# A convolution and feed-forward kernel: its first weight matrix loaded by channel group into 128 partitions, and sixteen closing matmuls left out

## The chip, the cores and the metric

The kernel runs on one core of a Trainium2 chip. The metric is the device time of one execution in microseconds (us). Before the change it is 2172.01 us, the median of three runs that lie between 2171.13 and 2172.34 us. TensorE (PE) does the matmuls, VectorE (DVE) and ScalarE (ACT) the elementwise work, GpSimd (POOL) and SyncE (SP) issue transfers here, and 16 DMA engines move the data.

## What is computed

```python
def _attn_ref(x, weight):                 # x: 8 x 4096 x 192, weight: 8 x 7
    w = softmax(weight, axis=-1)          # one causal filter of 7 taps for each of 8 heads
    # out[b, s, head, :] = sum over k of w[head, k] * x[b, s - 6 + k, head, :]

def _moe_ref(x, w_in, w_out):             # x: 32768 x 192, w_in: 192 x 2048, w_out: 2048 x 192
    h = x @ w_in
    g = h * (1.0 / (1.0 + np.exp(-1.702 * h)))
    return (g @ w_out).astype(np.float32)
```

`w_in` and `w_out` come as 64-bit floats, so the kernel has to turn them into 32-bit floats itself, from two 32-bit words for each number.

## The kernel before, in words

**Steady state.** The 32768 tokens are done in 32 rounds ("big") of 1024 tokens: two halves of 512 tokens in the two halves of the partitions. A round has a first product (x times `w_in`, lines L212 to L247), a gelu on ACT (L236), and a second product with `w_out` (L596, matmuls at L522), which is written as a long plan of forms that saves multiplications. For accuracy the first product takes three passes, over a high part, a low part and a difference of x (`xh`, `xl`, `xd`) with matching parts of the weights (`wh`, `wl`, and what is streamed through `ring`).

**The first round is special** (`first_step`, L713). The weights are not ready when it starts, so it works on four parts of `w_in`, each with 512 columns of the 2048: part i holds column blocks 2i and 2i+1 of 256 columns, one in partitions 0 to 63, the other in partitions 64 to 127. The 192 channels lie as three groups k of 64, side by side in each partition. `load_w_in(i)` (L324) loads part i into `raw[i]`, a region of the tile `g`; for part 0 it is called twice, for the left and the right half of the columns.

Each part then goes through the same steps. On DVE and ACT: `take` (L381, L382 on DVE; it is the first to read the loaded words), `clamp` (L387, L388 on ACT), `join` (L396, L401 on DVE), `rounded_in` (L409 on DVE). Part 0 is used as it is by `plain` (matmuls at L706). Parts 1 to 3 go on through `top` (ACT, L434), `rest` (DVE, L437), `spread` (ACT, L444) and `differ` (DVE, L448), and are used by `quick` (matmuls at L697). PE takes the products in 16 groups; groups 4i to 4i+3 belong to part i, and of these the last two need x with its two partition halves exchanged.

**The exchanges** (L687) are transfers from SBUF to SBUF that swap the two halves of the partitions: `own` and `xt` (x itself), later `xl` into a region of `wh`, and `xd` into a region of `wl`. Channel group 2 of `own` itself comes through such an exchange, so `xh`, `xl` and `xd` wait for one too.

**What sets the order.** The order of each engine is the order of the code. All the loads of `w_in`, all the exchanges, the later loads of `w_out` (L332) and the puts of weights to memory (L458) are issued by SP, in this order: x, `load_w_in(0)` (left, then right half), `load_w_in(1)`, the exchanges of `own` and `xt`, `load_w_in(2)`, `load_w_in(3)`, the exchange of `xl`, the exchange of `xd`, a load of `w_out`, the puts, more loads of `w_out`. On DVE, `take` of part 2 stands ahead of `rest` of part 1, and `take` of part 3 stands ahead of `join` of part 2.

**The end.** After the last round 16 matmuls follow (L902 to L909) whose results nobody reads: twelve of 128 rows by 512 columns and four that use half of the rows.

Of the kernel before, what the change touches and what calls it, by code (L numbers as in the profile page):

```python
# [10 lines left out]
U32 = mybir.dt.uint32  # L11
# [5 lines left out]
def kernel(  # L17
# [9 lines left out]
    nc = tc.nc  # L27
# [8 lines left out]
    NC = D // R  # L36
# [23 lines left out]
    halves = [slice(0, R), slice(R, P)]  # L60
# [23 lines left out]
    def flat_g(r):  # L84
        return g[:, r].rearrange("p n o i t -> p (n o i t)")
# [32 lines left out]
    xh, xl, xd = (consts.tile([P, 2 * NC, T], F32R, name=f"x{i}") for i in "hld")  # L118
# [63 lines left out]
    wh = consts.tile([P, NF // 2, NC, 2, P], F32R)  # L182
# [27 lines left out]
    KS = (1, 2, 0)  # L210
# [84 lines left out]
    raw = [flat_g(r)[:, 2 * PART * i : 2 * PART * (i + 1)] for r, i in ((0, 0), (1, 0), (2, 0), (2, 1))]  # L295
# [21 lines left out]
    w_in_v = moe_w_in.bitcast(U32).rearrange("(k q) (j f) -> j q k f", q=R, j=N_W)  # L317
# [4 lines left out]
    SETS = ((0, 4), (1, 5), (2, 4), (3, 5), (1, 2), (6, 7), (4, 5), (6, 7))  # L322

    def load_w_in(i, cols=slice(0, 4 * P)):  # L324
        for o in range(2):
            nc.sync.dma_start(  # L326
                out=raw[i][halves[o], :].bitcast(U32).rearrange("p (k f) -> p k f", k=NC)[:, :, cols],
                in_=w_in_v[2 * i + o][:, :, cols],
            )

    def load_w_out(i):
# [7 lines left out]
    for r in range(2):  # L339
        load_w_in(0, slice(2 * P * r, 2 * P * (r + 1)))  # L340
    load_w_in(1)

    nc.gpsimd.memset(sel, 1.0)
    for c in range(NC):
        part = sel[:, c, :].rearrange("i (h q) -> i h q", h=2)
        for sign in (1, -1):
            nc.gpsimd.affine_select(
                out=part,
                in_=part,
# [363 lines left out]
    def first_step(tiles):  # L713
# [34 lines left out]
        for i in range(2, N_IN):  # L748
            load_w_in(i)
# [123 lines left out]
    for big in range(1, N_BIG):  # L873
# [24 lines left out]
        pf, pa, pb, pc = tiles[3], tiles[1], tiles[0], tiles[2]  # L898
        begin = lambda: unit(big + 1, [pf], 0)
        second(big, pb, pa, pc, more, begin if more else lambda: None)  # L900
        tiles = [pf, pa, pb, pc]
    for i in range(14):  # L902
        if i in (8, 9):
            for o in range(2):
                nc.tensor.matmul(  # L905
                    pf[o], wh[halves[o], 0, 0, 0, :], xh[halves[o], 0:2, :], start=True, stop=True, skip_group_check=True
                )
        else:
            nc.tensor.matmul(pf[0], wh[:, 0, 0, 0, :], xh[:, 0:2, :], start=True, stop=True)  # L909


# [28 lines left out]
```

## Time and profile before

| What | Number |
|---|---|
| median of three runs | 2172.01 us |
| the profiled execution's own time | 2172.57 us |
| its span, first to last instruction | 2170.5 us |
| PE busy | 2165.7 us, 100% of the span |
| DVE, ACT, POOL busy | 82%, 46%, 15% |
| granted PE clock | 1.00 |
| data moved | 335.76 MB, of it 189.28 MB on the queue of SP |
| end of the first matmuls of the second product | from 55.3 us on |

The page has the busy share of each engine in 40 slices, the DMA queues with their packets and bytes, and a chain of work that is followed back from the last instruction. In lists of groups a row reads: line, engine, operation, written tile <- read tiles, partitions x elements, count. A row of the DMA issues reads: tiles, issuing engine, count, KB of one (of 1024 bytes), median us from issue to landing. The DMA share counts packets in flight, so that it can go somewhat over 1.

### The profile page before, as it was taken

The numbers are of one execution on the slowest core, as the hardware profiler recorded it, in microseconds if no ns is written. First come the engines' busy times: TensorE is split into PE (matmuls) and PEld (weight loads), VectorE is DVE, ScalarE is ACT, GpSimd is POOL, SyncE is SP. The second block draws the span as 40 slices with busy tenths as digits, with TensorE's granted clock in tenths as the row PEclk, the third lists the DMA queues.
The fourth block names the chain that finished last, engine by engine and source line by source line (L and its number), as shares of the span: only waits on it lengthen the run. The fifth ranks groups of instructions, "written<-read, shape, count | busy, mean of one in ns | idle before, by whom it ended". The sixth has DMA issues, their size and how long they took to land.

```text
span 2170.5 us, 66567 instructions
## 1 busy us (share of the span) xinstructions
PE 2165.7 (100%) x29126; PEld 1523.2 (70%) x29126; DVE 1775.2 (82%) x2501; ACT 990.7 (46%) x2116; POOL 324.2 (15%) x439
## 2 busy tenths in 40 slices
PE   9999999999999999999999999999999999999999
PEld 7567776677766777766777667776667776677766
DVE  7988888788888888887888878888888888787856
ACT  8344444444444444444444444444444444444443
POOL 0111111101111011111111110111101111111000
PEclk9999999999999999999999999999999999999999
DMA  9857576676666676656757657666667565676544
GB/s 243 216 126 186 146 165 137 142 168 159 162 144 139 153 176 153 154 135 140 185 147 165 137 138 170 163 160 144 142 147 178 150 158 138 140 181 150 138 112 104
DMA packets 266931, 335.76 MB, mean 155 GB/s; under 512 B 121296, under 2 KB 229728, under 8 KB 266512
## 3 DMA queue, kind: packets, MB, share of 16 engines
q0 software_dynamic: 42048, 141.83, 32.7%
q1 hardware_dynamic: 222944, 189.28, 31.8%
q8 instruction: 228, 3.74, 0.7%
q10 hardware_dynamic: 1648, 0.39, 0.1%
q14 instruction: 63, 0.52, 0.1%
HBM read 199.43 MB, written 29.88 MB: 106 GB/s over the span
## 4 chain that ended last, share of the span: by engine, by line
PE 99%; DMA 1%; DVE 0%; SPq 0%; issue 0%; DVEq 0%
PE slot L522 50%; PE slot L215 47%; PE slot L697 1%; PE slot L671 0%; DMA g<-in_moe_w_in_dram 0%; DMA g<-in_x_dram 0%; PE slot L909 0%; PE slot L706 0%; DVE xd L178 0%; SPq L137 0%; DVE w_form L437 0%; PE slot L905 0%; SPq L326 0%; DVE w_form L381 0%; DVE xt L143 0%
## 5 line engine op out<-in xcount | busy, mean ns | idle before, releaser
L522 PE MATMUL slot<-g,w_form 128*32 128x256 f32 x8928 | 894.1, 379 | 0.0
L238 ACT ACTIVATE g<-slot 128x512 f32<-128x512 f32 x1024 | 556.1, 597 | 500.8 <-PE slot L215 500.8
L585 DVE TENSOR_TENSOR g<-g 128x1024 f32<-128x1024 f32 x403 | 483.7, 1219 | 212.9 <-ACT g L238 114.5
L522 PEld LDWEIGHTS slot<-g,w_form 128*32 128x32 f32 x8928 | 479.7, 110 | 138.4
L633 ACT COPY room<-slot 32x256 f32<-32x256 f32 x651 | 239.0, 367 | 626.6 <-PE slot L522 624.4
L522 PE MATMUL slot<-g,w_out_s 128*32 128x256 f32 (+1 forms) x6336 | 509.2, 392 | 0.0
L215 PE MATMUL slot<-xh,wh 64*128 64x512 f32 x2976 | 422.4, 389 | 0.0
L215 PE MATMUL slot<-xd,ring 64*128 64x512 f32 x2976 | 418.3, 386 | 0.0
L522 PEld LDWEIGHTS slot<-g,w_out_s 128*32 128x32 f32 x6336 | 263.7, 110 | 195.3 <-issue 28.9
L164 DVE SCALAR_TENSOR_TENSOR own<-xt,cw,own 128x512 f32<-128x512 f32 (+1 forms) x546 | 362.8, 733 | 0.2
L215 PEld LDWEIGHTS slot<-xh,wh 64*128 64x128 f32 x2976 | 276.4, 184 | 70.0 <-issue 13.2
L215 PEld LDWEIGHTS slot<-xd,ring 64*128 64x128 f32 x2976 | 278.7, 184 | 58.8
L590 POOL DMA_DIRECT2D g<-g x124 | 117.6, 949 | 758.3 <-PE slot L522 518.9
L522 PE MATMUL slot<-osbs,w_form 128*32 128x256 f32 x2232 | 225.3, 379 | 0.0
L137 POOL DMA_DIRECT2D g<-in_x_dram x232 | 152.7, 666 | 401.4 <-PE slot L522 395.8
L215 PE MATMUL slot<-xl,wl 64*128 64x512 f32 x1488 | 209.4, 386 | 0.0
L215 PE MATMUL slot<-xl,ring 64*128 64x512 f32 x1488 | 209.0, 386 | 0.0
L522 PE MATMUL slot<-room,w_form 128*32 128x256 f32 x2232 | 171.5, 379 | 0.0
L215 PEld LDWEIGHTS slot<-xl,wl 64*128 64x128 f32 x1488 | 139.4, 184 | 30.1
L215 PEld LDWEIGHTS slot<-xl,ring 64*128 64x128 f32 x1488 | 139.4, 184 | 29.4
L522 PEld LDWEIGHTS slot<-osbs,w_form 128*32 128x32 f32 x2232 | 117.3, 110 | 42.7 <-ACT room L636 0.3
L585 DVE TENSOR_TENSOR room<-slot,room 96x256 f32<-96x256 f32 x248 | 100.1, 414 | 57.1 <-PE slot L522 55.0
(121 smaller groups left out, 1371.9 us busy)
## 6 DMA issues: line engine op xcount, KB each, us to landing
ring<-w_dram SPq DMA_DIRECT2D x744, 192.0 KB, 3.2
g<-g POOLq DMA_DIRECT2D x124, 512.0 KB, 6.9
g<-in_x_dram POOLq DMA_DIRECT2D x220, 180.0 KB, 4.2
out_dram<-osbs SPq DMA_DIRECT2D x186, 128.0 KB, 2.9
g<-osbs POOLq DMA_DIRECT2D x31, 512.0 KB, 5.8
g<-room POOLq DMA_DIRECT2D x31, 512.0 KB, 6.6
w_dram<-ring SPq DMA_DIRECT2D x14, 288.0 KB, 5.5
room<-in_x_dram SPq DMA_DIRECT2D x16, 180.0 KB, 5.9
```

The lines of the kernel that those rows point to most:

```text
L137: queue.dma_start(out=xin[q0 : q0 + Q, n, j:NJ, :], in_=x_v[n, p, t : t + (NJ - j) * Q, v * Q : v * Q + XW].rearrange("(j i) d -> i j d", ...
L164: vec.scalar_tensor_tensor(out=dst, in0=src, scalar=tap, in1=dst, op0=ALU.mult, op1=ALU.add)
L215: nc.tensor.matmul(slot[o], w(o)[halves[o], k, :], t[halves[o], 2 * k : 2 * k + 2, :], start=first and k == KS[0], stop=last and k == KS[- ...
L238: act.activation(g[:, r // NG, :, o, r % NG, :], slot[o].rearrange("p (n t) -> p n t", n=2), AF.Gelu_apprx_sigmoid,)
L522: nc.tensor.matmul(dst, w, t, start=first, stop=last, skip_group_check=True)
L585: (eng.tensor_add if op == "+" else eng.tensor_sub)(v(dst), v(a), v(b))
L590: nc.gpsimd.dma_start(out=spot(dst), in_=spot(a), accum_op=ALU.add)
L633: act.copy(to, d)
L697: nc.tensor.matmul(tiles[2 * h + r][h ^ s], w[halves[h], c, :], xs[s][halves[h], 2 * c : 2 * c + 2, :], start=n == 0 and c == KS[0], stop= ...
```

## The change

`load_w_in` issues three transfers for each call in place of two. Before, transfer o took one column block of the part into one half of the partitions, with all three channel groups (64 partitions x 3 rows). Now transfer k takes one channel group of both column blocks into all 128 partitions (128 rows). The bytes and the length of a row (256 words in the two calls for part 0, 512 words otherwise) stay. On the memory side the pattern was 64 x 3 x columns; it is now 2 x 64 x columns, with the two column blocks outermost, since a step from block to block cannot be merged with a step from channel to channel. On the other side it is 128 x columns. The 16 closing matmuls are left out as well.

```diff
     def load_w_in(i, cols=slice(0, 4 * P)):
-        for o in range(2):
+        for k in KS:
             nc.sync.dma_start(
-                out=raw[i][halves[o], :].bitcast(U32).rearrange("p (k f) -> p k f", k=NC)[:, :, cols],
-                in_=w_in_v[2 * i + o][:, :, cols],
+                out=raw[i].bitcast(U32).rearrange("p (k f) -> p k f", k=NC)[:, k, cols],
+                in_=w_in_v[2 * i : 2 * i + 2][:, :, k, cols],
             )
...
         second(big, pb, pa, pc, more, begin if more else lambda: None)
         tiles = [pf, pa, pb, pc]
-    for i in range(14):
-        if i in (8, 9):
-            for o in range(2):
-                nc.tensor.matmul(
-                    pf[o], wh[halves[o], 0, 0, 0, :], xh[halves[o], 0:2, :], start=True, stop=True, skip_group_check=True
-                )
-        else:
-            nc.tensor.matmul(pf[0], wh[:, 0, 0, 0, :], xh[:, 0:2, :], start=True, stop=True)
```

`w_in_v` is the view of `w_in` as (column block j, channel q within its group, channel group k, word f), and `KS` is (1, 2, 0).

SP's program near its start, before (-) and now (+); `g` is the tile that holds the raw weights, `in_moe_w_in_dram` is `w_in` in memory, and the numbers are the shape on the side that is written:

```order
 L137 DMA g<-in_x_dram 32x9x160 x2
-L326 DMA g<-in_moe_w_in_dram 64x3x256 x4
-L326 DMA g<-in_moe_w_in_dram 64x3x512 x2
+L326 DMA g<-in_moe_w_in_dram 128x1x256 x6
+L326 DMA g<-in_moe_w_in_dram 128x1x512 x3
 L687 DMA own<-xt 64x2x256 x2
 L687 DMA xt<-own 64x256 x2
 L687 DMA xt<-own 64x2x256 x2
-L326 DMA g<-in_moe_w_in_dram 64x3x512 x4
+L326 DMA g<-in_moe_w_in_dram 128x1x512 x6
 L687 DMA wh<-xl 64x1536 x2
 L687 DMA wl<-xd 64x512 x6
```

Ten loads of `w_in` have become fifteen, at the same places: the exchanges of L687 stand behind the loads of parts 0 and 1, and those of `xl` and `xd` behind the loads of parts 2 and 3, as they did.

The end of PE's program, before (-) and now (the first rows of what is gone; `slot` are the accumulators):

```order
 L522 MATMUL slot_65<-g,w_out_s 32x256 x3
 L522 MATMUL slot_66<-g,w_form 32x256
-L909 MATMUL slot_67<-xh,wh 128x512 x8
-L905 MATMUL slot_67<-xh,wh 128x512
-L905 MATMUL slot_68<-xh,wh 128x512
```

The last matmul of the last product is now the last matmul of the program. No other engine's order has changed.

## The prediction

> **What bounds the kernel now.** I read the totals first, then the chain of work that ended last, then the stretch at the start in which the changed transfers run. The first line of the page says that TensorE never stands still for long, and the chain shows where it does:
>
> ```profile
> PE 2165.7 (100%) x29126; PEld 1523.2 (70%) x29126; DVE 1775.2 (82%) x2501; ACT 990.7 (46%) x2116; POOL 324.2 (15%) x439
> ```
>
> ```profile
> 7.09 10.12 PE slot L671 x168
> 17.20 1.94 PE slot L706 x8
> ...
> 20.04 6.78 DMA g<-in_moe_w_in_dram
> ...
> 26.91 0.56 DVE w_form L381
> ...
> 31.21 24.11 PE slot L697 x200
> 55.32 4.84 PE slot L522 x40
> ```
>
> From 31.21 us to the end the chain is matmuls alone. Whatever the start gains or loses up to about 31 us therefore passes undiminished to the end, and nothing else of the change can. Ahead of that the chain leaves PE once: it goes through a load of `w_in` (landing at 26.82 us) and DVE's `take` of part 2 at 26.91 us. So the loads of `w_in` are on the path that sets the end, with little to gain: the whole detour from the load to 31.21 us hides behind matmuls but for some 2 us, in which the weight loads of PE wait (1.3 + 0.8 us in the first 60 us):
>
> ```profile
> PEld slot L697 <- ACT wl L444: 1.3, 1, 1.3
> ...
> PEld slot L697 <- DVE xd L178: 0.8, 2, 0.4
> ```
>
> **Which engines a transfer uses.** The question that decides the case is how the new transfers are shared out over the 16 DMA engines. The small queue q10 (ACT's) shows how this is done. It carries the load of the taps (8 rows of 7 words) in the first 10 us, and six stores of 64 KB at the end:
>
> ```profile
> q10 hardware_dynamic: 16, 0.00, 0.1%
> ...
> w<-in_weight_dram ACTq DMA_DIRECT2D x1, 0.2 KB
> ```
>
> ```profile
> q10 hardware_dynamic: 1632, 0.39, 17.5%
> ...
> out_dram<-osbs ACTq DMA_DIRECT2D x6, 64.0 KB, 1.9
> ```
>
> A store has 32 x 8 rows of 256 bytes, 256 packets; 1632 / 6 is 272, so 16 packets close it, one for each engine. The taps make 16 packets for 8 rows: 8 close it. A transfer whose outermost count is 8 thus ran on 8 engines, one whose outermost count is 32 on all 16: the outermost count is what is shared out. Every load of `w_in` so far has 64 outermost on both sides. The new ones have 128 on the side of SBUF, but 2 on the side of memory (two column blocks, then 64 channels). I infer that the smaller side decides, so that each new transfer runs on 2 engines, one for each column block. No row of before has two unequal sides; this is the step that I am least sure of.
>
> The Trainium skill's "DMA: Bandwidth & Descriptors" (section "Why a DMA increments its semaphore by 16 and not by 1") says that the engine count is the largest number up to 16 that divides the slowest dimension above 1 on both sides, and its "Rules for kernel authors" warn that an outermost size c below 16 confines a transfer to c engines; the 8 closing packets of the taps agree.
>
> **The rate of an engine.** Three stretches of full DMA share, for all 16 engines together:
>
> ```profile
> 2.00:7.80 5.80, 4.69 (x31) 4.34 (x34) 1.97 (x8) 4.62 (x15) 1.58 (x8) 1.00 1.13 240
> ...
> 23.00:28.00 5.00, 5.00 (x26) 4.00 (x26) 2.46 (x5) 4.17 (x6) 0.00 (x0) 1.00 1.09 228
> 36.00:40.00 4.00, 4.00 (x34) 3.07 (x35) 4.00 (x7) 3.21 (x7) 0.00 (x0) 1.00 1.05 383
> ```
>
> The last two columns are the DMA share and GB/s. From 23 to 28 us the old loads of `w_in` run (rows of 2 KB into one half of the partitions), at 228 / 16 = 14.3 GB/s for an engine. From 36 to 40 us `w_out` is loaded into all 128 partitions (rows of 1.5 KB), at 383 / 16 = 23.9 GB/s. Since the shorter rows are the faster, the rows are not what slows `w_in`; the half of the partitions is. Two engines that write one half each have room to spare there, so I take 23.9, the nearest row, and keep 14.3 as the slow end. The fast end is 446 / 16 = 27.9, the best tenth of a microsecond between 36 and 40 us:
>
> ```profile
> GB/s 369 384 399 353 338 415 384 384 323 369 353 384 369 369 338 369 446 384 384 415 369 415 338 369 430 369 415 399 369 430 384 399 384 415 399 415 323 446 323 384
> ```
>
> "DMA: Bandwidth & Descriptors" of the Trainium skill gives about 27 GiB/s for an engine ("Specifications"), which is 29.0 GB/s; by that the sum below would come to about 2204.5 us instead, just under the fast end.
>
> **The sum.** These are the transfers on SP's queue that the two engines must do in their order:
>
> ```profile
> g<-in_moe_w_in_dram SPq DMA_DIRECT2D x6, 384.0 KB, 7.0
> ...
> g<-in_moe_w_in_dram SPq DMA_DIRECT2D x4, 192.0 KB, 5.5
> ...
> wh<-xl SPq DMA_DIRECT2D x2, 384.0 KB, 9.8
> wl<-xd SPq DMA_DIRECT2D x6, 128.0 KB, 4.5
> ...
> own<-xt SPq DMA_DIRECT2D x2, 128.0 KB, 2.3
> ...
> xt<-own SPq DMA_DIRECT2D x2, 128.0 KB, 3.5
> ...
> xt<-own SPq DMA_DIRECT2D x2, 64.0 KB, 2.0
> ```
>
> The weights are 6 x 384 + 4 x 192 = 3072 KB or 3145.7 kB, half of it for each engine: 1572.9 kB. The exchanges of `own` and `xt` are 640 KB, those of `xl` and `xd` 768 KB each; they spread over 16 engines, so engine 0 or 1 has 41.0 and 98.3 kB of them. The first 7.8 us go to x as before: 240 GB/s from 2.0 to 7.8 us are 1392 kB, which is all of x (4 x 180 + 4 x 160 KB). From 7.8 us on each of the two engines has 1572.9 + 41.0 + 98.3 = 1712.2 kB in a row, without a gap: SP issues the later loads long before the first are through, as it does now:
>
> ```profile
> 15.31 1.29 SPq L687 DMA_DIRECT2D own<-xt  x2
> 16.71 2.61 SPq L687 DMA_DIRECT2D xt<-own  x4
> 19.37 3.35 SPq L326 DMA_DIRECT2D g<-in_moe_w_in_dram  x4
> 22.82 1.19 SPq L687 DMA_DIRECT2D wh<-xl  x2
> ```
>
> At 23.9 GB/s that is 71.6 us, so the exchange of `xd`, the last of the row, lands at 79.4 us. On the way part 0 lands near 24 us, part 1 near 41, the exchange of `own` behind it near 42, part 2 near 59 and part 3 near 75. PE stands still after the convolution for most of this: it cannot end the first product before the exchange of `own`, groups 4 and 5 wait for part 2 (DVE has its `take` ahead of `rest` of part 1), and groups 6 and 7 wait for the exchanges of `xl` and `xd`. From 79.4 us on it still has to do the third pass of group 6, group 7 and two passes of group 8 before it stands where it now stands at 39.92 us:
>
> ```profile
> 34.97 1.87 PE L697 MATMUL slot<-wl,ring 64*128 64x512 f32 x6
> 36.35 1.21 PE L697 MATMUL slot<-wh 64*128 64x512 f32 x6
> ...
> 38.55 1.07 PE L697 MATMUL slot<-xh,wh 64*128 64x512 f32 x6
> 39.24 1.06 PE L697 MATMUL slot<-xl,wl 64*128 64x512 f32 x6
> 39.92 1.07 PE L697 MATMUL slot<-xd,ring 64*128 64x512 f32 x6
> ```
>
> Six passes start 0.69 us apart, 4.1 us. So it is there at 83.5 us, 43.6 us later. The other way, through DVE, gives nearly the same:
>
> ```profile
> 31.55 0.55 DVE L381 TENSOR_SCALAR w_form<-g 128x768 uint32<-128x768 uint32 x1
> ...
> 39.16 0.55 DVE L448 TENSOR_TENSOR ring<-ring,wh 128x384 fp32r<-128x384 f32 x1
> ```
>
> `take` of part 3, at 31.55 us now, can start at 75.3, and the last `differ` of part 2 follows 7.6 us behind it either way, some 43 us later than now. From there on the order and the durations are the old ones; the loads of `w_out`, behind the exchanges on the same queue, are spread over 16 engines and keep their distance.
>
> Two small terms. The first matmuls of the kernel, after idling, take longer than later ones of the same shape:
>
> ```profile
> L483 PE MATMUL slot<-osbs x11: 275/421/421, 2.7 to 5.7; 128*128 128x128 f32 x11
> ```
>
> 421 against 275 ns for some 3.6 us (1.42 to 5 us) is 1.2 us, once after the last wait: between 0 and 1.2, and I take 1.2. The closing matmuls take PE to 2169.15 us:
>
> ```profile
> 2165.22 2.14 PE L909 MATMUL slot<-xh,wh 128*128 128x512 f32 x8
> ...
> 2167.95 1.20 PE L909 MATMUL slot<-xh,wh 128*128 128x512 f32 x4
> ```
>
> ```profile
> L519 ACTq DMA_DIRECT2D out_dram<-osbs x6: 323/373/463, 2163.7 to 2167.5; - x6
> ```
>
> The last store is issued at 2167.5 us and lands 1.9 us later, at 2169.4, so the stores cover them: I take 0.3 us off, between 0 and 0.5. If that cover were gone, PE would end 3.9 us earlier.
>
> 43.6 + 1.2 - 0.3 = 44.5 us, on the profiled execution's own 2172.57 us: **2217.1 us** (this execution lies 0.56 us above the median, which changes nothing here). At 27.9 GB/s the row is 61.4 us and the sum 33.4 us plus at most 0.9: 2206. At 14.3 it is 119.7 and the sum 92: 2265.
>
> **The rivals.**
> *All 16 engines after all.* If the 128 of the SBUF side (or both outer counts of the memory side together) are shared out, the load fills 128 partitions and runs at 383 instead of 228 GB/s. Its place is `take` of part 2: 786 kB land 1.4 us earlier, `rest` starts 1.3 us earlier (it then waits for `top`), PE's waits of about 2 us near 29 to 31 us shrink by 1.2, with the closing 0.3: 2171.1 us. It is not slower, and it decides if DMA share stays near 1.1 and GB/s above 228 from 8 to 14 us. For it speaks that 128 partitions are plainly the faster shape; against it the closing packets of the taps. The Trainium skill's rules for kernel authors on the same page call for one 128-partition transfer in place of two half ones, which is this outcome.
> *The same rate, more issues.* Sixteen engines, 228 GB/s, but three issues for a part in place of two, at the 0.61 us of this row: part 2 lands 0.6 us later, 2173 us.
>
> ```profile
> L326 SPq DMA_DIRECT2D g<-in_moe_w_in_dram x10: 607/612/1367, 4.7 to 22.1; - x10
> ```
>
> *Two engines, limited by themselves.* If an engine does 14.3 GB/s on these rows wherever they go, it is 2265 us; against it, the 1.5 KB rows at 23.9.
>
> **How the numbers follow.** Two engines 0.86 (of this 0.10 near the slow end), 16 engines faster 0.11, same rate 0.02, something that gains more 0.01. About 0.2%, 4.3 us, is what a measurement of this kernel can tell from no change; the start holds no more than 2 us to gain, so both 16-engine cases are within it. Faster 0.01, same 0.13, slower 0.86. The range takes the two ends of the rate with the few microseconds that the passes are uncertain by, 2203 to 2266; it holds all but 0.05 of the first case, 0.81.
>
> **What would show it.** Right: DMA share of 0.1 to 0.2 and some 48 GB/s from 10 to 75 us, landing times of L326 that grow from transfer to transfer to tens of microseconds, PE idle by 40 us in total before 84 us, waiting on L687 and on DVE behind L381, and then the same chain of matmuls at the same durations. Wrong: loads of `w_in` that land in 3 to 6 us, with the chain's long wait near 20 us shorter. A store that lands after 2169 us plus the shift shows the closing matmuls as covered.

## The result, and the profile after

The changed kernel takes 2218.99 us (median of five runs, 2217.95 to 2219.22) against 2172.01 us: the ratio is 1.0217, with a 95% interval of 1.0206 to 1.0229. The profiled execution took 2219.21 us, with a span of 2217.1 us, 46.6 us longer than before. First the totals and the 40 slices of the page:

```profile
PE 2170.2 (98%) x29110; PEld 1521.0 (69%) x29110; DVE 1775.1 (80%) x2501; ACT 990.7 (45%) x2116; POOL 325.2 (15%) x439
...
PE   5799999999999999999999999999999999999999
...
PEclk8799999999999999999999999999999999999999
DMA  2776676666575666675666675766675766675544
GB/s 79 207 196 139 141 180 152 162 145 142 138 185 149 162 146 141 143 183 145 164 142 145 144 179 147 165 137 145 150 176 147 166 141 141 154 174 148 137 112 106
```

But for the 16 matmuls the engines do the same work as before, though PE is busy 4.5 us longer. All that has changed stands in the first two slices (0 to 111 us): PE is busy half of the first one, and the DMA engines move 79 GB/s there, where it was 243. The stretches show why (the last two columns are DMA share and GB/s, the one before them the granted PE clock):

```profile
8.00:24.00 16.00, 8.61 (x155) 7.03 (x147) 3.42 (x8) 2.99 (x13) 0.00 (x0) 0.90 0.14 49
...
42.00:57.00 15.00, 10.60 (x46) 8.60 (x42) 4.45 (x4) 6.93 (x9) 0.00 (x0) 0.84 0.13 52
```

A share of 0.13 to 0.14 is two engines of 16 and a little, and 49 to 52 GB/s is 24.5 to 26 GB/s for each. So it goes on until 77 us, but for the bursts in which the exchanges use all 16 engines. The rows of DVE's `take`, the first of each part of `w_in`, with the idle time ahead of it:

```profile
24.79 0.42 DVE L381 TENSOR_SCALAR w_form<-g 128x384 uint32<-128x384 uint32 x1 [13.26 <-DMA g<-in_moe_w_in_dram]
...
40.71 0.56 DVE L381 TENSOR_SCALAR w_form<-g 128x768 uint32<-128x768 uint32 x1 [10.63 <-DMA g<-in_moe_w_in_dram]
...
57.93 0.56 DVE L381 TENSOR_SCALAR w_form<-g 128x768 uint32<-128x768 uint32 x1 [10.40 <-DMA g<-in_moe_w_in_dram]
...
77.02 0.56 DVE L381 TENSOR_SCALAR w_form<-g 128x768 uint32<-128x768 uint32 x1 [14.37 <-DMA g<-in_moe_w_in_dram]
```

Parts 0 to 3 are there at about 25, 41, 58 and 77 us (24, 41, 59 and 75 were forecast). PE has a wait behind each, 40.2 us in all (40 were forecast), the last for the exchange of `xl` behind part 3, with 10.9 us at a stretch:

```profile
28.00 3.48 PE L706 MATMUL slot<-own,w_form 64*128 64x512 f32 x8 [11.39 <-DVE w_form L409]
41.05 5.70 PE L706 MATMUL slot<-own,w_form 64*128 64x512 f32 x16 [9.57 <-DMA own<-xt]
...
60.43 1.65 PE L697 MATMUL slot<-xl,wl 64*128 64x512 f32 x6 [7.84 <-ACT wl L444]
...
66.18 0.86 PE L697 MATMUL slot<-wh 64*128 64x512 f32 x6
77.89 0.79 PE L697 MATMUL slot<-wh,wl 64*128 64x512 f32 x1 [10.85 <-DMA wh<-xl]
79.19 1.64 PE L697 MATMUL slot<-wh,wl 64*128 64x512 f32 x5 [0.52 <-DMA wh<-xl]
80.22 2.18 PE L697 MATMUL slot<-wl,ring 64*128 64x512 f32 x6
81.79 1.89 PE L697 MATMUL slot<-wh 64*128 64x512 f32 x6
83.07 1.89 PE L697 MATMUL slot<-wh,ring 64*128 64x512 f32 x6
84.35 1.68 PE L697 MATMUL slot<-wl,ring 64*128 64x512 f32 x6
85.63 0.87 PE L697 MATMUL slot<-xh,wh 64*128 64x512 f32 x5
...
87.02 0.39 PE L697 MATMUL slot<-xd,ring 64*128 64x512 f32 x1
```

The last row is the point that stood at 39.92 us before: 47.1 us later. From there the chain is matmuls with the old durations, but for the first stretch of L522, which is 0.5 us shorter. Before:

```profile
55.32 41.88 PE slot L522 x384
```

After:

```profile
102.39 41.34 PE slot L522 x384
```

That leaves the 46.6 us.

### The profile page after: what moved, and what is told of

The parts are those of the page before. It is cut to its first block, busy times and chain, and to the rows that moved or that the text cites. A ratio compares the mean times of both kernels' runs of the same rounds, so it can differ in the third digit from the quotient of the medians.

```text
span 2217.1 us, 66543 instructions
## 1 busy us (share of the span) xinstructions
PE 2170.2 (98%) x29110; PEld 1521.0 (69%) x29110; DVE 1775.1 (80%) x2501; ACT 990.7 (45%) x2116; POOL 325.2 (15%) x439
## 4 chain that ended last, share of the span: by engine, by line
PE 96%; DMA 2%; SPq 1%; DVE 0%; issue 0%; DVEq 0%
PE slot L522 49%; PE slot L215 46%; DMA g<-in_moe_w_in_dram 2%; PE slot L697 1%; SPq L326 1%; DMA wh<-xl 1%; SPq L137 0%; SPq L687 0%; DVE xd L178 0%; DVE ring L448 0%; DVE osbs L509 0%; DVE w_form L437 0%; DVE room L585 0%; DVE w_form L381 0%; DVE w_form L382 0%
## 5 line engine op out<-in xcount | busy, mean ns | idle before, releaser
L522 PE MATMUL slot<-g,w_form 128*32 128x256 f32 x8928 | 894.1, 379 | 0.0
L522 PEld LDWEIGHTS slot<-g,w_form 128*32 128x32 f32 x8928 | 479.7, 110 | 138.4
L522 PE MATMUL slot<-g,w_out_s 128*32 128x256 f32 (+1 forms) x6336 | 508.7, 392 | 0.0
L522 PEld LDWEIGHTS slot<-g,w_out_s 128*32 128x32 f32 x6336 | 254.0, 110 | 204.5 <-issue 38.2
L522 PE MATMUL slot<-osbs,w_form 128*32 128x256 f32 x2232 | 225.3, 379 | 0.0
L522 PE MATMUL slot<-room,w_form 128*32 128x256 f32 x2232 | 171.5, 379 | 0.0
L522 PEld LDWEIGHTS slot<-osbs,w_form 128*32 128x32 f32 x2232 | 117.4, 110 | 42.6
```

The costliest lines, as they stand in the source:

```text
L522: nc.tensor.matmul(dst, w, t, start=first, stop=last, skip_group_check=True)
```

## The experiments

Eleven kernels, each timed against the kernel before on the same chip; the medians of before are 2171.27 to 2171.41 us there.

**Half-partition transfers by channel group.**

```diff
         for k in KS:
-            nc.sync.dma_start(out=raw[i]...[:, k, cols], in_=w_in_v[2 * i : 2 * i + 2][:, :, k, cols])
+            for o in range(2):
+                nc.sync.dma_start(out=raw[i][halves[o], :]...[:, k, cols], in_=w_in_v[2 * i + o][:, k, cols])
```

> The changed kernel, but each of the three transfers of a call is cut in two, one for each column block into its 64 partitions; outermost count 64 on both sides, six issues for a part. Two-engine theory: the slowdown is gone, 2172 to 2175 us (PE takes up part 1 near 27 us as before; up to 3 us for issues of 0.6 us that hold up the exchange of xl by some 3.8 us), full DMA share near 230 GB/s from 8 to 14 us. Rival, that loading by channel group or with more transfers is what costs: near 2219 us or above.

2176.61 us, ratio 1.0026 (1.0016 to 1.0035). Nearly the whole slowdown is gone, though there are more transfers, by channel group too. The 5 us that are left are a little more than expected, and the stretch from 8 to 14 us shows a term that had been missed:

```profile
8.00:14.00 6.00, 6.00 (x108) 5.31 (x104) 3.41 (x8) 2.89 (x13) 0.00 (x0) 1.00 0.44 122
```

With 64 KB for 0.6 us of issue, SP cannot feed 16 engines: half the share and half the rate, so every part lands later.

**Only the first two parts by the new transfers.**

```diff
+        if i < 2:
             for k in KS:      # as changed
                 ...
+        else:
+            for o in range(2):      # as before
+                ...
```

> The changed kernel with parts 2 and 3 loaded as before, parts 0 and 1 by the new transfers. Two-engine theory: at the 50 GB/s of the changed kernel part 1 and the exchange of own land near 41 to 42 us as there, but parts 2 and 3 follow within some 8 us, so PE waits once and then works on from where it stood at 19 us before: 2172.6 + 22 - 2 for waits that it had + 2 for a slow clock, 2192 to 2198 us. Rival, that each wait of PE behind a load adds a cost of its own and the bytes do not matter: no value between is singled out, but the saving against 2219 should then be about half the waits, 2 of 4, 2195 to 2205.

2193.96 us, ratio 1.0106 (1.0091 to 1.0121): inside the range that was worked out from the bytes, and 1 us under the rival's. Half of the bytes on two engines, somewhat less than half of the loss. The interval reaches from 2191 to 2198 us, so this time alone does not decide between the two.

**The old transfers, cut at 57 rows, and at 48.**

```diff
         for o in range(2):
-            nc.sync.dma_start(out=raw[i][halves[o], :]..., in_=w_in_v[2 * i + o][:, :, cols])
+            for q0, q1 in ((0, 57), (57, R)):      # or ((0, 48), (48, R))
+                nc.sync.dma_start(out=raw[i][o * R + q0 : o * R + q1, :]..., in_=w_in_v[2 * i + o][q0:q1, :, cols])
```

> The transfers of the kernel before (64 rows outermost, one half of the partitions), each cut into 57 and 7 rows, so that the outermost count is the same on both sides; closing matmuls left out. If the number of engines is the largest number up to 16 that divides the outermost counts, 57 = 3 x 19 runs on 3 engines and 7 on 7: each of the first three engines has 20 of 64 rows, 983 kB, plus 139 kB of exchanges, at 25 GB/s 44.9 us from 7.8 us on; shift 16.9 us and up to 3 us for a slow clock: 2188 to 2194 us. If the engines are only limited by the count itself (16 where it is 16 or more), 57 runs on 16: 2172 to 2175 us. If unequal sides alone confine a transfer, the same 2172 to 2175.

2197.23 us, ratio 1.0118 (1.0103 to 1.0133).

> The same cut at 48 and 16 rows, both multiples of 16: the control for the number of issues. By every theory of the engine count 16 engines: 2172 to 2174 us. If cutting itself costs, as much as with 57 and 7 rows.

2173.95 us, ratio 1.0012 (1.0003 to 1.0022). The two kernels issue the same number of transfers of equal outermost counts on both sides; 48 and 16 rows cost 2.6 us over the kernel before, 57 and 7 rows 26. The stretch from 8 to 20 us of the kernel with 57 rows:

```profile
8.00:20.00 12.00, 8.64 (x151) 7.22 (x142) 4.37 (x12) 3.38 (x14) 0.00 (x0) 1.00 0.24 81
```

Three engines have 60 of every 64 rows (3 x 19 of the 57, and one each of the 7), 76 of the 81 GB/s, 25.3 for each: about the rate that two engines have in the changed kernel. Sixteen would have moved 228 or more. So a count well above 16 can leave most engines idle; what counts is a common divisor.

The time is 3 us above the range. The sum put the bytes of the exchanges at 25 GB/s for each engine too, and that is too fast. From 45 to 49 us, while exchanges run, all sixteen together move 194 GB/s, 12 for each:

```profile
45.00:49.00 4.00, 3.83 (x20) 2.63 (x22) 2.38 (x5) 3.97 (x8) 0.00 (x0) 0.61 1.02 194
```

As an estimate from this row, 139 kB at that rate take 11.5 us in place of 5.6. That this is all of the difference is not shown.

**128 rows that follow each other in memory.**

```diff
+        rows = moe_w_in.bitcast(U32).rearrange("c (j f) -> j c f", j=N_W)
         for k in KS:
-            nc.sync.dma_start(out=raw[i]...[:, k, cols], in_=w_in_v[2 * i : 2 * i + 2][:, :, k, cols])
+            c0 = R * min(k, 1)
+            nc.sync.dma_start(out=raw[i]...[:, k, cols], in_=rows[2 * i + k % 2, c0 : c0 + P, cols])
```

> The changed kernel, but each transfer reads 128 channels that follow each other in memory, of one column block, in place of 64 channels of two blocks: the same three transfers of 128 rows with the same bytes, outermost count 128 on both sides. The weights then stand in the wrong places, so this kernel computes with a jumbled w_in; nothing else is left out. If only the outermost count of 2 is at fault, 16 engines run at about 383 GB/s from 8 us on and part 2 lands some 1.4 us earlier than in the kernel before: 2170.5 to 2171.5 us. If three transfers of one channel group into 128 partitions are slow in themselves: well above 2173 us.

2171.82 us, ratio 1.0003 (0.9994 to 1.0011). Three transfers of one channel group into 128 partitions are not slow; with 128 outermost on both sides the 46.6 us are gone. The transfers are faster, too: 349 GB/s at a share of 1.09 from 8 to 12 us (383 were expected; the kernel before moves 238 from 8 to 14). Yet the gain that this should have brought is not there. Part 2 is taken at 24.62 us, 2.3 us earlier than before (1.4 were expected), but PE then waits for something else, the exchange of `xl`:

```profile
24.62 0.56 DVE L383 TENSOR_SCALAR w_form<-g 128x768 uint32<-128x768 uint32 x1 [1.07 <-DMA g<-in_moe_w_in_dram]
```

```profile
32.60 0.49 PE L699 MATMUL slot<-wh,wl 64*128 64x512 f32 x1 [0.43 <-DMA wh<-xl]
33.48 0.96 PE L699 MATMUL slot<-wh,wl 64*128 64x512 f32 x5 [0.39 <-DMA wh<-xl]
```

The second product starts at 55.16 us, against 55.32 before.

**The closing matmuls, both ways:** put back into the changed kernel, and left out of the kernel before (the diffs are the second half of the change).

> The changed kernel with the 16 closing matmuls back. If the last stores cover them: 2219 us, no more than 0.5 us above the changed kernel. If they cost what they take on PE, 3.9 us more, 2223 us.

> The kernel before without the 16 closing matmuls and nothing else. Covered by the last stores: 2171.5 to 2172.1 us. Rival, that they end the program: 2168 us.

2219.07 us, ratio 1.0218 (1.0204 to 1.0232), and 2171.47 us, ratio 1.0000 (0.9991 to 1.0009). They cost nothing that can be told, in either kernel; the 3.9 us of the rivals lie outside the intervals. What covers them is seen in SP's waits at the end, here of the kernel before without them, where it waits for the stores as long as ever (with them the same row has 1.5, 2, 1.0):

```profile
SPq L927 <- DMA out_dram<-osbs: 1.6, 2, 1.0
SPq L927 <- PEq L927: 0.7, 2, 0.5
```

**PE kept busy ahead of the last wait**, with 36 and with 50 added matmuls.

```diff
-        products(5, 6)
+        products(5)
+        for _ in range(36):      # or 50
+            nc.tensor.matmul(tiles[1][1], wh[:, 1, 0, 0, :], xh[:, 0:2, :], start=True, stop=True)
+        products(6)
         gelus(5, 6)
```

> The changed kernel with 36 matmuls of 128 rows by 512 columns put between the products of groups 5 and 6, into an accumulator that group 7 starts afresh (work that nobody reads is added, nothing is left out), so that PE does not idle for 10.9 us ahead of the last wait. If the slow passes after that wait (1.28 us apart in place of 0.69, five of them) come from the lowered clock after idling, they return to 0.69 and the time falls by 2 to 3 us, to 2216 to 2217 us. If they are slow for another reason (operands that arrive late), no change or up to 1 us slower, 2219 to 2220 us.

2218.39 us, ratio 1.0216 (1.0202 to 1.0230).

> As the run with 36 added matmuls ahead of group 6, but 50, so that PE is busy until just ahead of the landing of xl at 79.2 us and the clock is not lowered again in the 2 us before it (added work that nobody reads, nothing left out). If the clock is what makes the passes after the wait slow: passes 0.69 us apart from 79.3 us on, the third pass of group 8 at 84 us in place of 87.0 (85.8 with 36), 2216 to 2217 us. If they are slow for another reason: 2218 to 2220 us.

2218.07 us, ratio 1.0216 (1.0200 to 1.0232). The gain, 0.6 and 0.9 us by the medians, is below what was expected. Against the kernel before that was timed beside each, it is 0.0 and 0.2 us (the changed kernel is 47.0 us slower, these two 47.0 and 46.8), which is nothing that the times can tell. The trace is plainer. From 80 to 85 us, first the changed kernel, then the one with 50:

```profile
80.00:85.00 5.00, 5.00 (x24) 3.90 (x24) 5.00 (x7) 3.40 (x6) 0.00 (x0) 0.50 1.00 316
```

```profile
80.00:85.00 5.00, 5.00 (x38) 3.70 (x37) 5.00 (x7) 3.44 (x7) 0.00 (x0) 1.00 1.00 324
```

The granted clock is 0.50 and 1.00 (the column ahead of the DMA share), the matmuls that start in these 5 us are 24 and 38, and all but the first of the passes are 0.68 to 0.79 us apart again:

```profile
79.79 2.03 PE L697 MATMUL slot<-wl,ring 64*128 64x512 f32 x6
81.32 1.18 PE L697 MATMUL slot<-wh 64*128 64x512 f32 x6
82.11 1.06 PE L697 MATMUL slot<-wh,ring 64*128 64x512 f32 x6
82.79 1.06 PE L697 MATMUL slot<-wl,ring 64*128 64x512 f32 x6
...
84.83 1.06 PE L697 MATMUL slot<-xd,ring 64*128 64x512 f32 x6
```

So the slow passes are the clock, and the point that was at 87.02 us comes at 84.83. But about half of these 2.2 us is lost again: the first product ends 1.7 us earlier (L522 starts at 100.70 us, not 102.39), and the first stretch of L522 takes 41.84 us, not 41.34. PE's weight loads now wait 1.2 us for the gelu of ACT, a wait that the trace of the changed kernel does not have behind 82 us:

```profile
PEld slot L697 <- DMA wl<-xd: 0.8, 3, 0.3
PEld slot L522 <- ACT g L238: 0.7, 2, 0.4
PEld slot L697 <- ACT g L238: 0.5, 2, 0.3
```

The first row belongs to the first pass above. It takes 1.5 us at the full clock as well, since `xd` comes in while it runs; that part of the delay is not the clock.

**The exchanges on another queue.**

```diff
-    def exchange(dst, src, queue=nc.sync):
+    def exchange(dst, src, queue=nc.gpsimd):
```

> The changed kernel with all exchanges issued by POOL on its own queue in place of SP's. If the exchanges wait behind the weights because they share SP's queue and its order: own and xt are exchanged near 20 us, long before part 1 lands, and those of xl and xd land some 3 to 6 us after they are ready; the end is then set by take of part 3 near 75 to 77 us and differ of part 2 7.6 us later, 1 to 4 us less than 2219 us. If the exchanges are slow because engines 0 and 1 are busy whatever the queue, they land late as now: 2219 us.

2222.64 us, ratio 1.0236 (1.0222 to 1.0250): slower than the changed kernel by 3.7 us, which neither theory expected. The first half of the expectation holds in part: the exchange of `own` is issued at 27.71 us, not near 20, but it lands ahead of part 1, and PE goes on with it 7.7 us earlier:

```profile
33.34 5.88 PE L706 MATMUL slot<-own,w_form 64*128 64x512 f32 x15 [1.70 <-DMA own<-xt]
```

What was overlooked is that the exchanges' bytes still cross the same two engines. On SP's queue those of `xl` and `xd` come behind part 3; on a queue of their own they are issued from 45.70 and 65.61 us on and go ahead of it, 98.3 kB or, as an estimate, at least 3.9 us at 25 GB/s for each engine. Part 3 is taken 5.3 us later, at 82.36 us:

```profile
82.36 0.56 DVE L381 TENSOR_SCALAR w_form<-g 128x768 uint32<-128x768 uint32 x1 [14.83 <-DMA g<-in_moe_w_in_dram]
```

**A better place for one load**, in the kernel before without its closing matmuls:

```diff
-            nc.sync.dma_start(
+            (act if (i, o) == (2, 1) else nc.sync).dma_start(
```

> The kernel before without the closing matmuls, the second transfer of part 2 issued by ACT in place of SP, so that it is issued 1.5 to 2 us earlier and does not stand behind the exchanges on SP's queue. If the landing of part 2 sets when PE goes on at 31 us: up to 1 us gained, 2170.5 to 2171.5 us. If the issue on ACT delays the copies that xh waits for as much, no change, 2171.5 us, or up to 0.6 us slower.

2171.30 us, ratio 1.0001 (0.9992 to 1.0010): nothing gained. The load of part 2 has left the chain of waits, and the exchange of x has taken its place:

```profile
18.60 5.34 DMA xt<-own
```

No version came out ahead of the kernel before.

## Why the prediction was right, step by step

- **Two engines.** Right, and shown from three sides: 49 to 52 GB/s at a share of 0.13 to 0.14; the return to 2171.82 us with 128 rows outermost on both sides; and 57 rows, which run on three. The last corrects the wording: the prediction said that the smaller side decides. With 57 on both sides it is the largest divisor up to 16 that sets the count. By the Trainium skill's "DMA: Bandwidth & Descriptors" ("Why a DMA increments its semaphore by 16 and not by 1") that is the rule, for the two sides together; 2 and 128 give 2 by either wording, so that the sum was not touched.
- **The rate of an engine.** 23.9 GB/s was taken from the loads of `w_out`; 24.5 to 26 was measured while the two engines had the weights alone. The slow end, 14.3, is refuted as a limit of an engine on these rows: the kernel with 57 rows fills the same half of the partitions with the same rows, and its engines do 25.3. (The stretch that 14.3 was read from, 23 to 28 us, also carries the exchange of `xl`, issued from 22.82 us on; from 8 to 14 us, with `w_in` alone, the kernel before moves 238 GB/s, 14.9 for each.) That sixteen engines get in each other's way in one half fits this, and so do the 349 GB/s of the kernel with 128 rows, but no run shows it by itself.
- **The row of transfers.** 71.6 us were forecast from 7.8 us on, to the landing of the exchange of `xd` at 79.4 us. PE's weight loads wait for `xd` for the last time until 81.2 us, so the row took about 73.4 us. That it came so close is partly luck, for two misses offset each other: with the weights alone the engines are faster than 23.9, and while the exchanges run they are slower (220 GB/s for all sixteen from 66 to 71 us, 13.8 for each). So part 2 came 1 us earlier than forecast and part 3 nearly 2 us later. The prediction also had SP issue the later loads long ahead, and it does not (the last exchange of `xd` is issued until 77.4 us). The row has no gap all the same: from 8 to 80 us the DMA share of no microsecond is below 0.12.
- **The way from there.** Six passes at 0.69 us, 4.1 us, with 1.2 us more for a slow clock. They took 6.8 us (80.22 to 87.02). At the full clock, with 50 added matmuls, they take 5.0 us (79.79 to 84.83); the 0.9 us over the forecast are the first pass, in which `xd` comes in, as it did in the kernel before (34.97 to 36.35 us in the prediction's own rows). The slow clock costs 1.8 us here and 0.4 us ahead of 80.22, 2.2 us in all. This term was mis-sized: three starts of passes lie 1.28 us apart, and the low clock lasts longer than the 3.6 us taken from the kernel's first matmuls (a granted clock of 0.50 from 78 to 85 us, 0.89 from 85 to 88). The runs with added matmuls show that it is the clock, and their traces that only about 1 us of it reaches the end.
- **The closing matmuls.** 0.3 us were taken off; the two runs show nothing.
- **The sum.** 43.6 + 1.2 - 0.3 = 44.5 us forecast. Measured are 43.6 us, 1.3 for the late `xd` (at the full clock the point of group 8 stands at 84.83 us, where 83.5 was forecast) and 2.2 for the clock, 47.1 us at group 8; less 0.5 in the next stretch that is 46.6 us.
- **The rival with 16 engines** failed on its condition, and would have failed on its gain: the run with 128 rows had the early landing, but its second product starts only 0.2 us earlier, where 1.2 was forecast, with PE's next wait, for `xl`, in the place of the old one.

## What to carry to other kernels

Before a transfer is reshaped, write down the outermost count of its pattern on both sides: here a destination of 128 partitions was worth nothing, as the source could only be written with 2 outermost, and a count of 57 on both sides left three engines, where 48 and 16 cost only 2.6 us. What stood behind the slow transfers on the queue and touched all engines, the exchanges, waited as well, and moving them to another queue only changed who waits. Ask also what a faster load would leave as the last wait; here the next one, for `xl`, ended at 33.48 us, when the old one had ended at 31.21.

## What the runs showed beyond that

SP itself is held up. The first two new loads are issued in 0.69 and 0.53 us, the next ones take 2.6 us each, which is the time that an engine needs for 64 rows of 1 KB at 25 GB/s (65.5 kB):

```profile
4.72 0.69 SPq L326
...
5.46 0.53 SPq L326
...
6.04 2.54 SPq L326
...
8.62 2.62 SPq L326
...
11.29 2.63 SPq L326
```

An issue waits, it seems, until the engines have drained an earlier transfer, so an engine that only issues transfers is no longer free to run ahead. How many may be under way was not measured.
